# Batch 0's keys without turning: maxima turned on TensorE, a diagonal product beside identity times keys, and a new order

## The chip, the cores and the metric

One core of one Trainium2 chip runs the whole kernel. The metric is the device time of an execution in microseconds (us); less is better. The core has TensorE (PE, matrix products; PEld loads its weights), VectorE (DVE), ScalarE (ACT), GpSimd (POOL) and SyncE (SP), whose queue issues nearly all DMAs here. Each engine works through its own queue in order and waits for others by semaphores.

## What is computed

The reference is a linear attention followed by a feed-forward layer with a maximum of three products. Cut to what matters:

```
q_s = softmax(q, over the 64 columns of a head)        # 8 batches, 8 heads, 576 rows, 64 columns
k_s = softmax(k, over the 576 rows)                    # a maximum and a sum per column
kv  = einsum('bhsd,bhse->bhde', k_s, v)
x   = einsum('bhsd,bhde->bhse', q_s, kv)               # 4608 x 512 when heads stand side by side
h   = max(x @ w1, x @ w2, x @ w3)                      # 512 -> 768
out = h @ w_out                                        # 768 -> 512
```

Everything is float32. The softmax of the keys runs along the rows, which lie on the partitions of the chip's memory, so its maximum and sum go across partitions.

## The kernel before, in words

**The work and its tiles.** The 576 rows of a batch are split into 512 ("main") and 64 ("left"). Attention goes by pairs of heads: a `Pair(b, g)` has number n = 4 b + g, and m = n % 2. Two pairs, m = 0 and m = 1, together give two of the four 128-row blocks of x (blocks `cc` 0 to 3 of a batch). The feed-forward layer multiplies each f32 number as a high and a low part, three products (`L985` for the gates, `L1032` for the second layer); the weights are split into such parts in twelve "slices" (`Slices`, lines 463 to 492) by ACT, DVE and POOL at the start. Batches 0 to 2 run gate by gate (`Chunk`), batches 3 and later in couples by a scheme with seven products instead of eight (`Duo`, L1211), whose mixed weights are prepared meanwhile (`mix_weights`, L1100 to 1110, over the buffer `bdf`).

**Keys of batches 0 and 1** go through `k_turned`: TensorE turns the keys of a pair (L620 and 624 in batch 0, L611 and 614 in batch 1), so that the maximum runs along the free axis on DVE (L629, L630); ACT takes the exponential with the maximum as bias and gathers the sum (L636, L637); TensorE turns the result back (L642, L643); ACT or DVE copies it (L647, L648); TensorE multiplies it with v (L716, ten products per pair); DVE makes the reciprocal of the sum (L722, L725) and ACT scales the two 64x64 results into the diagonal blocks of a 128x128 matrix of `bdf` (L728). `bdf` is cleared once at the start (L386). From batch 2 on, `k_plain` finds the maximum across partitions with POOL's all-reduce (L660).

**Queries.** For the pairs in `Q_BY_ACT`, ACT does exponential and sum row block by row block (L757, eight instructions of 64 columns, each followed by a read of its accumulator); for the others DVE or POOL subtracts the maximum (L762), ACT takes one exponential (L786) and DVE the sums (L788). From batch 2 on, `ROWS_FROM` to `ROWS_TO` says the same for later pairs (L775 against L781, L786, L788). Normalised queries (L802) of batches 0 and 1 are turned on TensorE (L839) and copied (L843).

**x.** L858 multiplies the queries with the matrices of `bdf`; ACT copies the high part (L865); the low part is made by TensorE and ACT for the blocks in `X_BY_PE` (L868: minus identity times the high part into the same bank, L870: copy), else by DVE (L873).

**The order.** Nothing is reordered on the chip: a planner in the kernel (`Streams`) writes out the order of every engine's queue before the run. Each stream of steps has a rank; a step whose inputs are ready by the planner's own costs is issued in order of time, and among those ready at about the same time the lowest rank goes first. Steps that name two engines go to the one that ends first. The constants `AT`, `STEP` (ranks of batches 0 and 1), `FIRST`, `CHUNK`, `PAIR_STEP` (later batches), `SLICE...` (weight slices), `LEFT_AT`, `KEEP_AT`, `MIX_AT` set these ranks. `FIRST_LOADS` is the written-out order of the first loads on SP's queue: `w` a weight slice (1 MB), `k`, `q`, `v` 512 rows of a pair (256 KB), `K`, `V` the left rows of two pairs (64 KB). While TensorE has nothing ready early on, the planner fills in products of the identity by itself (L415). Rooms such as four PSUM banks `pf` (gates and, in batch 0, the small results `sm`), three banks `pa` and one `sm` bound what can be under way; `in_pf` fixes the order in which `pf` is handed out.

Of the kernel before, what the change touches and what calls it, by code (L numbers as in the profile page):

```python
# [45 lines left out]

BANKS = 3, 1

Q_BY_ACT = (0, 2, 3, 4, 5, 7)

KEEP_AFTER = 'wo'

WO_AT = 185.58

BEFORE_Y0 = 6

X_BY_PE = (1, 2, 3)
# [45 lines left out]
class Streams:  # L103
# [3 lines left out]
    def __init__(self, rooms, queued):  # L107
        self.all, self.when, self.blocked, self.left = [], {}, {}, 0
        self.queued = queued
        self.rooms = rooms  # L110
        self.taken = {}
        self.freed = {}
        self.clock = {"S": 0.72, "A": 2.2, "V": 4.0, "G": 9.0, "T": 0.0, "-": 0.0}
# [129 lines left out]
def linear_attention_then_maxout_ffn(  # L243
# [121 lines left out]
    keT = start.tile([P, S], F32, name="keT", bufs=1)  # L365
    qf = [place(f"qf{i}", [P, CH], F32, E_AT + 28672 + 2048 * i) for i in range(2)]

    minus = place("minus", [P, P], F32R, H_AT + 10240)
    nc.gpsimd.memset(adder, 0)
    nc.gpsimd.tensor_add(out=adder[:, 0:1], in0=adder[:, 0:1], in1=adder[:, 1:2])  # L370
# [23 lines left out]
    def left_rows(src, b, hs):  # L394
        return src[b, hs, CH:S].rearrange("h p d -> p h d")

    in_pf = [("sm", n) for n in range(NP)]
# [12 lines left out]
    st = Streams({"pf": 4, "pa": BANKS[0], "sm": BANKS[1], "keT": 1, "hp": NJ, "tmp": 3, "ke": 2, "kep": 1, "qe": 2, "qf": 2, "qt": 1, "tb": 1, "qT": 1, "ws": len(ws), "hs": 3}, {"pf": in_pf, "hs": in_hs, "ws": in_ws, "tb": list(range(TURNED * NP, B * NP, 2))})  # L410
    spare = sm.tile([P, CH], F32, name="sm")

    def products_for_nothing(n):
# [98 lines left out]
    class Pair:  # L512
# [89 lines left out]
        def k_turned(self):  # L602
# [44 lines left out]
            copy(out=ke[:, 0:4].rearrange("p s h d -> p (s h d)"), in_=kep)  # L647
            copy(out=ke[:LEFT, 4].rearrange("p h d -> p (h d)"), in_=kel)  # L648

        def k_plain(self):  # L650
# [24 lines left out]
            if n % 2:  # L675
                yield from self.two_products()
# [27 lines left out]
        def k_steps(self):  # L704
            n = self.n
            if not self.turned:
                yield from self.k_plain()
                return
            yield from self.k_turned()
            ke = self.ke  # L710
            yield Step("T", 0.9, [("v", n)], free=[("ke", n)], gives=("kv", n))
            kv = self.sm[:, 2 * P : 3 * P]
            for s in range(5):
                rows = slice(0, LEFT if s == 4 else P)
                for hh, r in enumerate(heads):
                    nc.tensor.matmul(  # L716
                        out=kv[r, :D], lhsT=ke[rows, s, hh, :], rhs=self.v_rest[rows, hh] if s == 4 else self.vt[rows, hh, s],
                        start=(s == 0), stop=(s == 4),
                    )
# [6 lines left out]
            yield Step("A", 0.65, free=[self.small_room()], gives=("bd", n))  # L726
            for r in heads:
                nc.scalar.activation(out=bdf[r, n, r], in_=kv[r, 0:D], func=AF.Copy, scale=rk[r])  # L728


        def q_steps(self):
# [113 lines left out]
        def x_steps(self):  # L845
# [10 lines left out]
            for m in range(2):  # L856
                for hh, r in enumerate(heads):
                    nc.tensor.matmul(  # L858
                        out=banks[hh][heads[m], :], lhsT=bdf[r, n - 1 + m, r], rhs=qf[m][r, :], start=True, stop=True
                    )  # L860
            for hh in range(2):
                cc = 2 * (self.g // 2) + hh
# [47 lines left out]
    def left_queries():  # L910
# [39 lines left out]
        for n in range(0, TURNED * NP, 2):  # L950
            b, g = divmod(n, NP)
            for m in range(2):
                for hh, r in enumerate(heads):
                    at, to = (g + m) * P + b * LEFT, g // 2 * P + b * LEFT
                    nc.tensor.matmul(
                        out=banks[hh][heads[m], to : to + LEFT], lhsT=bdf[r, n + m, r], rhs=qT[r, at : at + LEFT],
                        start=True, stop=True,
                    )
        for hh in range(2):
# [378 lines left out]
                yield Step("S", 0.68, gives=(ch, g), kb=(256, 256))  # L1338
                nc.sync.dma_start(out=to[low][0:LEFT, hs, 4, :], in_=left_rows(of[low], 0, hs))

    def landed(g):
        for ch in "kqv":
            yield Step("-", 0.0, [("%smain" % ch, g), (ch.upper(), g // 2) if ch != "q" else None], gives=(ch, g))

    st.add(first_loads(), -1000.0)
    for g in range(NP):
        st.add(landed(g), 0.0)

    def open_late():
        yield Step("-", 0.0, [("x", 0, g) for g in range(NP)], gives="late")  # L1350
# [58 lines left out]
    for (b, g), p in pairs.items():  # L1409
# [10 lines left out]
        st.add(p.k_steps(), at, step)  # L1420
# [66 lines left out]
```

## Time and profile before

| what | value |
|---|---|
| runs of the kernel before | 653.18 us median of 3 (653.03 to 654.44) |
| the profiled execution, its own time | 654.29 us |
| its span in the trace | 652.5 us |
| PE busy | 636.5 us, 98% |
| DVE, ACT, POOL busy | 431.4, 291.3, 58.0 us |
| DMA | 135.96 MB, mean 208 GB/s |

A profile describes one execution. "Busy" is the time in which an engine had an instruction under way; a busy PE is not PE at its peak. A line such as L620 is a line of the kernel before. In a timeline the columns are start, duration, engine, line, operation and shapes; in the chain of waits they are start, length, and what the end of the program was waiting for at that time. Windows list, for each stretch of the span, the busy time of each engine with the number of its instructions. All times in the text are microseconds from the start of the span unless said otherwise.

### The profile page before, as it was taken

The numbers are of one execution on the slowest core, as the hardware profiler recorded it, in microseconds if no ns is written. First come the engines' busy times: TensorE is split into PE (matmuls) and PEld (weight loads), VectorE is DVE, ScalarE is ACT, GpSimd is POOL, SyncE is SP. The second block draws the span as 40 slices with busy tenths as digits, with TensorE's granted clock in tenths as the row PEclk, the third lists the DMA queues.
The fourth block names the chain that finished last, engine by engine and source line by source line (L and its number), as shares of the span: only waits on it lengthen the run. The fifth ranks groups of instructions, "written<-read, shape, count | busy, mean of one in ns | idle before, by whom it ended". The sixth has DMA issues, their size and how long they took to land.

```text
span 652.5 us, 10284 instructions
## 1 busy us (share of the span) xinstructions
PE 636.5 (98%) x3599; PEld 509.6 (78%) x3599; DVE 431.4 (66%) x768; ACT 291.3 (45%) x713; POOL 58.0 (9%) x67
## 2 busy tenths in 40 slices
PE   6999999999999998999999999999999999999997
PEld 5768787887877777778787778778888888888885
DVE  7999987567777888988488999742436702343420
ACT  5999644266545534643244464422224522213131
POOL 1134342210010001010000011000000000000000
PEclk9999999999999999999999999999999999999999
DMA  9986477497887788899999971866663236666121
GB/s 287 365 237 224 160 252 277 128 293 216 260 266 226 203 229 222 247 297 319 315 236 265 259 208 60 245 199 193 192 193 117 78 127 190 193 193 196 39 65 64
DMA packets 137411, 135.96 MB, mean 208 GB/s; under 512 B 46608, under 2 KB 105488, under 8 KB 136208
## 3 DMA queue, kind: packets, MB, share of 16 engines
q1 hardware_dynamic: 137280, 135.17, 69.0%
q8 instruction: 29, 0.48, 0.3%
q14 instruction: 22, 0.18, 0.1%
q10 hardware_dynamic: 80, 0.13, 0.1%
HBM read 95.16 MB, written 33.03 MB: 196 GB/s over the span
## 4 chain that ended last, share of the span: by engine, by line
PE 83%; DVE 9%; DMA 5%; ACT 2%; issue 1%; POOL 0%; SPq 0%; DVEq 0%; ACTq 0%
PE pf L1211 38%; PE pf L1032 20%; PE pf L985 18%; DMA bdf<-keep_w 2%; PE pa L690 2%; DMA qt<-in_q_dram 2%; PE pa L890 2%; DVE tb L810 1%; DMA wst<-in_moe_w_dram 1%; DVE xb L1144 1%; DVE m L997 1%; PE sm L716 1%; DVE wx L472 1%; DVE xf L1148 1%; PE pa L839 0%
## 5 line engine op out<-in xcount | busy, mean ns | idle before, releaser
L1211 PE MATMUL pf<-xb,ws 128*128 128x512 f32 x1134 | 260.8, 390 | 0.2 <-DVE mm L1244 0.2
L1211 PEld LDWEIGHTS pf<-xb,ws 128*128 128x128 f32 x1134 | 212.2, 188 | 45.0 <-DVE mm L1244 0.6
L985 PE MATMUL pf<-x,wa 128*128 128x512 f32 x648 | 155.1, 394 | 0.0
L985 PEld LDWEIGHTS pf<-x,wa 128*128 128x128 f32 x648 | 119.6, 188 | 27.7 <-issue 2.4
L1240 DVE TENSOR_TENSOR mm<-pf,mm 128x512 f32<-128x512 f32 x36 | 24.9, 692 | 86.4 <-PE pf L1211 86.1
L1032 PE MATMUL pf<-oh,hs 128*128 128x512 f32 x192 | 59.3, 390 | 0.0
L1259 ACT COPY pf<-pf 128x512 f32<-128x512 f32 x27 | 15.4, 571 | 85.6 <-PE pf L1211 85.4
L1053 ACT COPY m<-pf 128x512 f32<-128x512 f32 x31 | 18.2, 586 | 59.6 <-PE pf L1032 50.9
L660 POOL PARTITION_ALL_REDUCE kma<-km x24 | 20.6, 859 | 263.9 <-DVE km L657 226.4
L1032 PEld LDWEIGHTS pf<-oh,hs 128*128 128x128 f32 x192 | 36.1, 188 | 7.6
L478 POOL TENSOR_TENSOR wx<-wx,wst 128x512 int32<-128x512 int32 x24 | 33.0, 1397 | 67.4 <-DMA vt<-in_v_dram 16.7
L1032 PE MATMUL pf<-ol,hs 128*128 128x512 f32 x96 | 37.7, 393 | 0.0
L775 ACT ACTIVATE qt<-qt,qm 128x64 f32<-128x64 f32 x81 | 27.1, 337 | 11.6 <-DVE qm L771 11.6
L1252 ACT COPY u<-pf 128x512 f32<-128x512 f32 x27 | 15.9, 587 | 34.3 <-PE pf L1211 34.1
L810 DVE STREAM_TRANSPOSE tb<-qt 128x576 f32<-128x576 f32 x24 | 30.3, 1261 | 0.2
L997 DVE TENSOR_TENSOR m<-pf,m 128x512 f32<-128x512 f32 x36 | 24.8, 688 | 8.4 <-PE pf L985 8.1
L1032 PE MATMUL pf<-oh,mix 128*128 128x512 f32 x96 | 30.2, 395 | 0.0
L1032 PE MATMUL pf<-oh,h_l 128*128 128x512 f32 x72 | 28.3, 393 | 1.3 <-DVE h_l L1004 1.3
L1032 PE MATMUL pf<-ol,h_h 128*128 128x512 f32 x72 | 28.9, 401 | 0.4 <-ACT h_h L1000 0.4
L1032 PE MATMUL pf<-oh,h_h 128*128 128x512 f32 x72 | 28.1, 390 | 0.0
L771 DVE TENSOR_REDUCE qm<-qt 128x9 f32<-128x576 f32 x24 | 17.4, 745 | 14.2 <-DMA qt<-in_q_dram 14.0
L1299 DVE TENSOR_TENSOR hs<-mm,hs 128x512 fp32r<-128x512 f32 (+1 forms) x32 | 17.1, 551 | 13.1 <-ACT hs L1297 13.0
(169 smaller groups left out, 872.1 us busy)
## 6 DMA issues: line engine op xcount, KB each, us to landing
ws<-keep_s SPq DMA_DIRECT2D x108, 256.0 KB, 3.3
ws<-keep_a SPq DMA_DIRECT2D x81, 256.0 KB, 3.2
wst<-in_moe_w_dram SPq DMA_DIRECT2D x9, 1024.0 KB, 7.4
keep_a<-wa SPq DMA_DIRECT2D x12, 768.0 KB, 6.0
keep_s<-mix SPq DMA_DIRECT2D x9, 1024.0 KB, 5.3
vt<-in_v_dram SPq DMA_DIRECT2D x56, 128.0 KB, 3.8
qt<-in_q_dram SPq DMA_DIRECT2D x24, 288.0 KB, 4.5
qT<-tb SPq DMA_DIRECT2D x96, 72.0 KB, 3.9
```

The source lines that it names most:

```text
L478: nc.gpsimd.tensor_add(out=x.bitcast(I32)[:, at], in0=x.bitcast(I32)[:, at], in1=low.bitcast(I32)[:, at])
L660: nc.gpsimd.partition_all_reduce(kma, km, P, bass_isa.ReduceOp.max)
L771: nc.vector.tensor_reduce(out=qm, in_=rows3, op=ALU.max, axis=AX.X, negate=by_act)
L775: nc.scalar.activation(out=rows3[:, s, :], in_=rows3[:, s, :], func=AF.Exp, bias=qm[:, s : s + 1], accum_out=qs[:, s : s + 1],)
L810: nc.vector.transpose(out=tb[:, self.m].rearrange("p e (c s) -> p s e c", s=QS), in_=self.qt.rearrange("p s (e c) -> p s e c", e=2),)
L985: nc.tensor.matmul(out=ps, lhsT=l[:, cc, js], rhs=r, start=(cc == 0 and t == 0), stop=(cc == NC - 1 and t == 2))
L997: nc.vector.tensor_max(out=m, in0=self.m.pop((j, i)), in1=m)
L1032: nc.tensor.matmul(out=po, lhsT=l, rhs=r[:, j, :], start=(j == 0 and i == 0), stop=(j == NJ - 1 and i == 2))
L1053: nc.scalar.copy(out=o, in_=po)
L1211: nc.tensor.matmul(out=bank[on], lhsT=w[:, k, a], rhs=x[:, b, k], start=(i == 0 and p in ("P1", "P5")), stop=(i == 5), skip_group_check=True,)
L1240: nc.vector.tensor_max(out=m, in0=bank[on], in1=m)
L1299: nc.vector.tensor_tensor(out=o[:, 1, jj], in0=mm[:, h, jj, ts], in1=o[:, 0, jj].bitcast(F32), op=ALU.subtract)
```

## The change

For batch 0, two pairs at a time: DVE or POOL takes the maximum over the row blocks within a partition (`k_most`: 512, 256 and 256 elements), TensorE turns the two 128x128 results, DVE takes the (negated) maximum along the free axis and multiplies the identity with it into `diag`. In `k_exp`, per pair, TensorE puts identity times keys into a bank and adds `same` (a matrix of ones) times `diag`, which subtracts each column's maximum on every partition; ACT takes one exponential from the bank. In `k_sums` TensorE multiplies with v, and with a column of ones for the sums; DVE makes the reciprocals and scales. No keys of batch 0 are turned, nothing is turned back and no sum is gathered on ACT. Keys of batch 1 go as before, but all 64x64 matrices now lie in columns 0 to 63 of their place in `bdf` ("matrices in one place"), so that one ACT instruction scales both, and `bdf` is no longer cleared. The small results of batch 0 take two `pf` turns instead of four. The order of the first loads, the ranks, `Q_BY_ACT`, `X_BY_PE` and `ROWS_TO` are new.

```
-FIRST, CHUNK, SLICE = 156.28, 58.31, 0.38
-PAIR_STEP, LATE_STEP = 10.68, 2.24
-AT = (91.2, -134.6, -41.9, 150.9, 228.6, 248.4, 271.1, -101.1)
-STEP = (13.73, 6.2)
-SLICES_AT, SLICE_STEP, SLICE_HI, SLICE_LO = -70.75, -0.79, 10.62, -16.13
+FIRST, CHUNK, SLICE = -26.06, 64.81, 1.49
+PAIR_STEP, LATE_STEP = 10.7, 2.75
+AT = (133.8, -45.7, -88.8, 94.7, 169.3, 289.5, 356.3, -82.3)
+STEP = (13.86, 1.0)
+SLICES_AT, SLICE_STEP, SLICE_HI, SLICE_LO = -3.29, -1.07, 14.53, -11.66
-FIRST_LOADS = 'wkqvKkkwvKVqwqkqvVv'
+FIRST_LOADS = 'wkqKkqvkvwwVqqkvVKv'
-Q_BY_ACT = (0, 2, 3, 4, 5, 7)
+Q_BY_ACT = (0, 2, 4, 5, 7)
-WO_AT = 185.58
+WO_AT = 145.21
-X_BY_PE = (1, 2, 3)
+X_BY_PE = (0, 1, 2, 4)
-ROWS_FROM, ROWS_TO = 8, 17
+ROWS_FROM, ROWS_TO = 8, 15
-LEFT_AT, KEEP_AT, PLAIN_AT, MIX_AT, MIX_STEP = 27.6, 1671.48, 53.02, 356.43, -81.06
+LEFT_AT, KEEP_AT, PLAIN_AT, MIX_AT, MIX_STEP = -26.51, 1749.35, 18.42, 378.43, -149.99
-    nc.vector.memset(bdf, 0.0)
+    nc.vector.memset(same, 1.0)
+        def k_most(self):
...
+            e = yield Step(
+                "VG", (dve(512) + 2 * dve(256), pool(512) + 2 * pool(256)), [("k", n - 1), ("k", n)], take=[("km4", n)],
+                port="VG",
+            )
...
+            unit[e].tensor_tensor(out=half4, in0=k4[:, :, 0:2], in1=k4[:, :, 2:4], op=ALU.max)
+            unit[e].tensor_tensor(out=most, in0=h4[:, :, :, 0], in1=h4[:, :, :, 1], op=ALU.max)
...
+            for i in range(2):
+                at = slice(i * P, (i + 1) * P)
+                nc.tensor.transpose(out=kmT[:, at], in_=km4[:, at], identity=ident)
...
+            nc.vector.tensor_reduce(out=km, in_=kmT.rearrange("p (m c) -> p m c", m=2), op=ALU.max, axis=AX.X, negate=True)
...
+            nc.vector.tensor_tensor(
+                out=diag, in0=ident.unsqueeze(1).broadcast_to([P, 2, P]), in1=km.unsqueeze(2).broadcast_to([P, 2, P]),
+                op=ALU.mult,
+            )
+        def k_exp(self, i):
...
+            nc.tensor.matmul(
+                out=kp, lhsT=ident, rhs=k4[:, i::2, 0:4].rearrange("p h s d -> p h (s d)"), start=True, stop=False,
...
+            nc.tensor.matmul(
+                out=kp, lhsT=same, rhs=diag[:, i].rearrange("p (h d) -> p h d", h=2).unsqueeze(2).broadcast_to([P, 2, 4, D]),
...
+            nc.scalar.activation(
+                out=ke[:, 0:4].rearrange("p s h d -> p h s d"), in_=kp.rearrange("p (h s d) -> p h s d", h=2, s=4), func=AF.Exp
+            )
+        def k_sums(self):
...
+                for s in range(5):
+                    rows = slice(0, LEFT if s == 4 else P)
+                    nc.tensor.matmul(
+                        out=kv[:, i, D : D + 1], lhsT=p.ke[rows, s].rearrange("p h d -> p (h d)"), rhs=ones[rows],
+                        start=(s == 0), stop=(s == 4),
+                    )
...
+                out=bdf[:, n - 1 : n + 1, :D], in0=kv[:, :, :D], in1=rk.unsqueeze(2).broadcast_to([P, 2, D]), op=ALU.mult
...
-            for r in heads:
-                nc.scalar.activation(out=bdf[r, n, r], in_=kv[r, 0:D], func=AF.Copy, scale=rk[r])
+            nc.scalar.activation(out=bdf[:, n, :D], in_=kv[:, :D], func=AF.Copy, scale=rk)
...
+        if b == 0 and p.m:
+            st.add(p.k_most(), at, step)
+            for i in range(2):
+                st.add(p.k_exp(i), at + (2 + i) * step, step)
+        st.add(p.k_steps(), at + (5 * step if b == 0 else 0.0), step)
```

More of the change, by code (lines that the diff above doesn't have):

```diff
@@ L366, in linear_attention_then_maxout_ffn @@
     qf = [place(f"qf{i}", [P, CH], F32, E_AT + 28672 + 2048 * i) for i in range(2)]
+    half4 = place("half4", [P, 4, 2, D], F32, H_AT)
+    km4 = place("km4", [P, 2 * P], F32, H_AT + 2048)
+    diag = place("diag", [P, 2, P], F32, H_AT + 3072)
+    same = place("same", [P, P], F32, H_AT + 4096)
     minus = place("minus", [P, P], F32R, H_AT + 10240)
@@ L395, in left_rows @@
         return src[b, hs, CH:S].rearrange("h p d -> p h d")
-    in_pf = [("sm", n) for n in range(NP)]
+    in_pf = [("sm", n) for n in range(1, NP, 2)]
     for c in range(PAIRED):
@@ L409, in linear_attention_then_maxout_ffn @@
         in_pf += [("S", c, i) for i in range(4)] + [(c, "y", t) for t in range(8)]
-    st = Streams({"pf": 4, "pa": BANKS[0], "sm": BANKS[1], "keT": 1, "hp": NJ, "tmp": 3, "ke": 2, "kep": 1, "qe": 2, "qf": 2, "qt": 1, "tb": 1, "qT": 1, "ws": len(ws), "hs": 3}, {"pf": in_pf, "hs": in_hs, "ws": in_ws, "tb": list(range(TURNED * NP, B * NP, 2))})
+    st = Streams({"pf": 4, "pa": BANKS[0], "sm": BANKS[1], "keT": 1, "km4": 1, "diag": 1, "hp": NJ, "tmp": 3, "ke": 2, "kep": 1, "qe": 2, "qf": 2, "qt": 1, "tb": 1, "qT": 1, "ws": len(ws), "hs": 3}, {"pf": in_pf, "hs": in_hs, "ws": in_ws, "tb": list(range(TURNED * NP, B * NP, 2))})
     spare = sm.tile([P, CH], F32, name="sm")
@@ new lines, in k_exp @@
+        def k_exp(self, i):
+            n, k4 = self.n, k0[:, self.four : self.four + 4]
+            p = pairs[divmod(n - 1 + i, NP)]
+            room = [("pa", ("ke", p.n))]
+            yield Step("T", f32(CH) + f32(P), [("kmT", n)], take=room)
+            kp, kl = pa.tile([P, CH], F32, name="pa"), self.sm[:LEFT, (2 + i) * P : (3 + i) * P]
+            nc.tensor.matmul(
+                out=kp, lhsT=ident, rhs=k4[:, i::2, 0:4].rearrange("p h s d -> p h (s d)"), start=True, stop=False,
+                skip_group_check=True,
+            )
+            nc.tensor.matmul(
+                out=kl, lhsT=ident[:LEFT, :LEFT], rhs=k4[:LEFT, i::2, 4], start=True, stop=False, skip_group_check=True
+            )
+            yield Step("T", f32(CH) + f32(P), [("diag", n)], free=[("diag", n)] if i else ())
+            nc.tensor.matmul(
+                out=kp, lhsT=same, rhs=diag[:, i].rearrange("p (h d) -> p h d", h=2).unsqueeze(2).broadcast_to([P, 2, 4, D]),
+                start=False, stop=True, skip_group_check=True,
+            )
+            nc.tensor.matmul(out=kl, lhsT=same[:, :LEFT], rhs=diag[:, i], start=False, stop=True, skip_group_check=True)
+            yield Step("A", act(CH) + act(P), take=[("ke", p.n)], free=room, gives=("kexp", p.n))
+            ke = p.ke = att.tile([P, 5, 2, D], F32, name="ke")
+            nc.scalar.activation(
+                out=ke[:, 0:4].rearrange("p s h d -> p h s d"), in_=kp.rearrange("p (h s d) -> p h s d", h=2, s=4), func=AF.Exp
+            )
+            nc.scalar.activation(out=ke[:LEFT, 4].rearrange("p h d -> p (h d)"), in_=kl, func=AF.Exp)
@@ new lines, in k_sums @@
+        def k_sums(self):
+            n, both = self.n, (pairs[divmod(self.n - 1, NP)], self)
+            yield Step(
+                "T", 2.5, [("kexp", n - 1), ("kexp", n), ("v", n - 1), ("v", n), ("diag", n)], free=[("ke", n - 1), ("ke", n)],
+                gives=("kv", n),
+            )
+            kv = self.sm.rearrange("p (i c) -> p i c", c=P)[:, 0:2]
+            for i, p in enumerate(both):
+                for s in range(5):
+                    rows = slice(0, LEFT if s == 4 else P)
+                    for hh, r in enumerate(heads):
+                        nc.tensor.matmul(
+                            out=kv[r, i, :D], lhsT=p.ke[rows, s, hh, :], rhs=p.v_rest[rows, hh] if s == 4 else p.vt[rows, hh, s],
+                            start=(s == 0), stop=(s == 4),
+                        )
+                for s in range(5):
+                    rows = slice(0, LEFT if s == 4 else P)
+                    nc.tensor.matmul(
+                        out=kv[:, i, D : D + 1], lhsT=p.ke[rows, s].rearrange("p h d -> p (h d)"), rhs=ones[rows],
+                        start=(s == 0), stop=(s == 4),
+                    )
+            yield Step("V", 0.35)
+            rk = att.tile([P, 2], F32, name="rk2", bufs=2)
+            nc.vector.tensor_scalar_add(out=rk, in0=kv[:, :, D], scalar1=1e-9)
+            nc.vector.reciprocal(out=rk, in_=rk)
+            yield Step("V", dve(2 * D) + 0.05, gives=("bd", n), free=[self.small_room()])
+            nc.vector.tensor_tensor(
+                out=bdf[:, n - 1 : n + 1, :D], in0=kv[:, :, :D], in1=rk.unsqueeze(2).broadcast_to([P, 2, D]), op=ALU.mult
+            )
+            yield Step("-", 0.0, gives=("bd", n - 1))
@@ L708, in k_steps @@
                 return
+            if self.b == 0:
+                if self.m:
+                    yield from self.k_sums()
+                return
             yield from self.k_turned()
@@ L725, in k_steps @@
             nc.vector.reciprocal(out=rk, in_=rk)
[L726 to L728 removed]
+            yield Step("A", 0.35, free=[self.small_room()], gives=("bd", n))
+            nc.scalar.activation(out=bdf[:, n, :D], in_=kv[:, :D], func=AF.Copy, scale=rk)
         def q_steps(self):
@@ L858, in x_steps @@
                     nc.tensor.matmul(
-                        out=banks[hh][heads[m], :], lhsT=bdf[r, n - 1 + m, r], rhs=qf[m][r, :], start=True, stop=True
+                        out=banks[hh][heads[m], :], lhsT=bdf[r, n - 1 + m, :D], rhs=qf[m][r, :], start=True, stop=True
                     )
@@ L955, in left_queries @@
                     nc.tensor.matmul(
-                        out=banks[hh][heads[m], to : to + LEFT], lhsT=bdf[r, n + m, r], rhs=qT[r, at : at + LEFT],
+                        out=banks[hh][heads[m], to : to + LEFT], lhsT=bdf[r, n + m, :D], rhs=qT[r, at : at + LEFT],
                         start=True, stop=True,
@@ L1339, in first_loads, with landed @@
                 nc.sync.dma_start(out=to[low][0:LEFT, hs, 4, :], in_=left_rows(of[low], 0, hs))
-    def landed(g):
-        for ch in "kqv":
-            yield Step("-", 0.0, [("%smain" % ch, g), (ch.upper(), g // 2) if ch != "q" else None], gives=(ch, g))
+    def landed(g, ch):
+        yield Step("-", 0.0, [("%smain" % ch, g), (ch.upper(), g // 2) if ch != "q" else None], gives=(ch, g))
     st.add(first_loads(), -1000.0)
     for g in range(NP):
-        st.add(landed(g), 0.0)
+        for ch in "kqv":
+            st.add(landed(g, ch), 0.0)
     def open_late():
```

14 lines of the change are left out of this document (12 added, 2 removed).

## The prediction

> **What bounds the kernel now.** I read the page's span first, then the busy times by stretches, then the busy time of line 415 alone, and last the chain of waits.
>
> ```profile
> span 652.5 us, 10284 instructions
> ```
>
> ```profile
> 10.00:35.00 25.00, 21.90 (x240) 17.31 (x240) 22.02 (x49) 22.78 (x83) 6.51 (x7) 1.00 1.08 349
> 35.00:61.00 26.00, 25.56 (x180) 19.47 (x178) 24.64 (x45) 25.26 (x83) 8.05 (x8) 1.00 0.79 244
> 61.00:220.00 159.00, 158.81 (x976) 125.95 (x973) 121.19 (x220) 85.36 (x265) 30.73 (x36) 1.00 0.71 225
> 220.00:290.00 70.00, 66.76 (x385) 51.12 (x384) 63.18 (x117) 32.66 (x61) 5.42 (x6) 1.00 0.86 247
> 290.00:648.40 358.40, 358.33 (x1802) 290.70 (x1800) 193.01 (x320) 122.03 (x223) 7.04 (x8) 1.00 0.62 182
> ```
>
> The columns are the stretch, its length, and the busy time of PE, PEld, DVE, ACT and POOL. From 61 us on, PE is a queue that is always full: it idles 0.19 us up to 220, 3.24 us from 220 to 290 and 0.07 us up to 648.4. What happens early is therefore passed on to the end as long as the stretch at 220 to 290 lets it through. Before 61 us, PE's busy time is partly filler: products of the identity by itself (line 415) that are issued while nothing else is ready.
>
> ```profile
> 10.00:35.00 25.00, 8.83 (x61) 7.30 (x60) 1.00 1.08 349
> ```
>
> So of the 25 us from 10 to 35, PE works 21.90 - 8.83 = 13.07 us and has 11.9 us free; the 26 us from 35 to 61 hold eight records of filler, 0.89 us (the row at 38.68 further down), so 24.7 of work and 1.3 free. What sets the moment of the first gate product is DVE and ACT: 22.02 + 22.78 of 2 x 25 us busy, and 24.64 + 25.26 of 2 x 26 in the stretch behind it. The chain that ended last, in order of time, shows them one after the other up to the first x:
>
> ```profile
> 22.43 0.60 DVE ke L647
> ...
> 23.97 0.75 DVE keT L630
> ...
> 30.66 0.31 ACT bdf L728
> 30.99 0.78 ACT keT L636 x2
> ...
> 33.88 0.70 DVE x L873
> ```
>
> The first four rows are work on batch 0's keys that lies on this chain (line 647 copies the turned-back keys, 630 finds a maximum, 728 scales, 636 is the exponential): 0.60 + 0.75 + 0.31 + 0.78 = 2.44 us, and not all of it is shown. The last row is the low part of the first x, 0.70 us on DVE; the first gate product comes when it is written, at 34.6 to 35.
>
> **The change, part by part.** Prices are the step from one start to the next, where the engine ran on without a gap.
>
> *TensorE.*
>
> ```profile
> 38.68 0.89 PE sm L415 x8
> ...
> 42.96 1.02 PE pa L858 x8
> ...
> 47.45 0.88 PE sm L716 x20
> ```
>
> ```profile
> 15.23 0.66 PE L642 MATMUL pa<-ident,keT 128*128 128x128 f32 x4
> ...
> 15.93 1.09 PE L620 MATMUL pa<-ident,k 128*64 128x128 f32 x16
> ...
> 17.21 0.71 PE L415 MATMUL sm<-ident 128*128 128x128 f32 x4
> ```
>
> The old way costs per pair 17.21 - 15.93 = 1.28 us (turning the keys), 15.93 - 15.23 = 0.70 (turning back) and 0.88 (line 716): 2.86, and 11.4 for four pairs. The new products are in f32 with a moving side of 512 and 128 columns, which the trace doesn't have in this form. Ten products of line 716 show as 20 records, so one f32 product of 128 columns by 128 is two records of line 415, 2 x 0.89 / 8 = 0.22 us, and by columns one of 512 is 0.89. The other bound is line 858, four products of 512 columns in quarters of the array in 1.02 us, 0.26 each (it is also the x of pairs 2 and 3). The full array is line 415's form, so I take 0.89 + 0.22. For two pairs: identity by keys and `same` by `diag`, 2 x 2 x 1.11 = 4.44; two transposes 0.22; the sums over v 2 x 0.88 = 1.76; ten products with `ones` of one column, 20 records between nothing and 0.11 each, nearest to line 716's 0.88 / 20 = 0.044, so 0.9. That is 7.3, and 14.6 for the batch: 3.2 us more than before (with the ends, from 4.9 less to 5.8 more). One more low part of x goes over PE (X_BY_PE has four instead of three), at most 0.89. All of this is hidden by the 11.9 + 1.3 us that PE has free before 61 us, as long as it is issued there; if that cover is gone, it is 3.2 to 4 us on the end.
>
> *VectorE.*
>
> ```profile
> 21.75 0.68 DVE L788 TENSOR_REDUCE qs<-qe 128x8 f32<-128x512 f32 x1
> 22.34 0.69 DVE L647 COPY ke<-pa 128x512 f32<-128x512 f32 x1
> ...
> 28.20 0.69 DVE L647 COPY ke<-pa 128x512 f32<-128x512 f32 x1
> ...
> 28.99 0.20 DVE L629 TENSOR_REDUCE km<-pf 128x1 f32<-128x64 f32 x1
> ...
> 29.91 0.08 DVE L630 DVE_READ_ACCUMULATOR2_ANT km<- 128x1 f32 x1
> ```
>
> Old: maximum 29.91 - 28.99 = 0.92 per pair, copy 28.99 - 28.20 = 0.79 for two of the four pairs: 5.3 us. New, per two pairs: one maximum over 512 elements, 22.34 - 21.75 = 0.59 by the nearest row; two over 256 and the diagonal product, also 256.
>
> ```profile
> 216.27 0.42 DVE L1100 TENSOR_TENSOR bdf<-bdf 128x256 f32<-128x256 f32 x1
> 216.61 0.69 DVE L997 TENSOR_TENSOR m<-pf,m 128x512 f32<-128x512 f32 x1
> ...
> 217.99 0.76 DVE L781 TENSOR_TENSOR qt<-qt,qm 128x576 f32<-128x576 f32 x1
> 218.66 0.15 DVE L697 TENSOR_SCALAR rk<-pa 128x2 f32<-128x2 f32 x1
> ```
>
> The first two rows give 0.34 for 256 elements; the reduction of 256 lies between line 629's 0.20 (64 elements) and 0.59 (512), I take 0.40; the scaling of 128 is below 0.34, I take 0.25. Sum 0.59 + 3 x 0.34 + 0.40 + 0.25 = 2.26, twice 4.5: 0.8 us saved. The small reciprocals become two sets instead of four; I leave them at nothing. Pair 3's queries leave ACT's row-by-row form (Q_BY_ACT loses 3), which adds a subtraction and a sum on DVE, 2 x 0.59 = 1.2. X_BY_PE gains 0, and 4 for 3: one low part less, -0.70. Net: -0.3 us. The clearing of `bdf` at the start is dropped for a smaller memset; it lies in the time in which the weights are awaited, so nothing.
>
> GpSimd may take the three maxima instead, at the planner's choice. A row says that it isn't free of charge: line 802's product, which elsewhere has about line 788's length, took twice that when GpSimd was in its integer additions (first fence DVE, second POOL).
>
> ```profile
> 43.82 1.46 DVE L802 TENSOR_TENSOR qe<-qe,qs 128x512 f32<-128x512 f32 x1
> ```
>
> ```profile
> 42.17 2.55 POOL L478 TENSOR_TENSOR wx<-wx,wst 128x512 int32<-128x512 int32 x2 [5.88 <-DVE km L629]
> ```
>
> [...]
>
> *ScalarE.*
>
> ```profile
> 14.41 0.68 ACT L636 ACTIVATE keT<-pa,km 128x512 f32<-128x512 f32 x1
> ...
> 15.37 1.15 ACT L463 ACTIVATE wx<-wst 128x1024 f32<-128x1024 f32 x1
> ...
> 20.56 0.63 ACT L786 ACTIVATE qe<-qe 128x512 f32<-128x512 f32 x1
> 21.08 1.18 ACT L482 ACTIVATE wst<-wst 128x1024 int32<-128x1024 uint32 x1
> 22.15 0.34 ACT L757 ACTIVATE qe<-q,qm 128x64 f32<-128x64 f32 x1
> ...
> 24.81 1.03 ACT L486 CAST wa<-wx 128x1024 fp32r<-128x1024 f32 x1
> ```
>
> Old: exponential and its sums 15.37 - 14.41 = 0.96, scaling two times 0.31 per pair (line 728 in the chain), and two copies at 0.79 (DVE's row, the nearest shown): 4 x 1.58 + 1.58 = 7.9 us. New: one exponential of 512 without a sum, 21.08 - 20.56 = 0.52, and one of 128 below the 0.31 of line 728's scaling, I take 0.27: 3.2. Saved 4.7. Pair 3's queries: 24.81 - 22.15 = 2.66 becomes 0.52, 2.1 saved. Batch 1 scales with one instruction for two: 4 x 0.31 = 1.2. The additional low part over PE costs a copy, 0.52. Net: -7.5 us.
>
> *Sum for the start.* If nothing is rebalanced, the head shrinks by DVE's 0.3 us. If the planner's choices (which of ACT and DVE takes the sign bits, the copies) even both engines out, it is (7.5 + 0.3) / 2 = 3.9. The chain's rows alone say: 2.44 of keys and 0.70 of x leave it, and 2.26 of new DVE work, that of two pairs, comes in their place: 0.9, a floor, since not all that leaves is shown. I take 2.2, between the bounds.
>
> *The order of loads.* The sequence is written out anew. The last rows of keys 2 and 3 (`K`, second) were tenth and are now 18th of 19, where the second `V` stood, whose row this is:
>
> ```profile
> L1339 SPq DMA_DIRECT2D v<-in_v_dram x2: 596/602/607, 7.8 to 15.1; - x2
> ...
> DMA to landing us min/median/max: 6.4/7.8/8.1
> ```
>
> Issued at about 15.1 and landed 6.4 to 8.1 us later, they are there at 21.5 to 23.2. Keys 2 and 3 can't begin earlier. The x of pairs 2 and 3 was multiplied at 42.96; from 23 it has 20 us left, and its DVE, PE and ACT work is 2.26 + 7.3 + 1.6 + 1.0 = 12.2. Nothing, then, unless other work goes first (below).
>
> *The later order.* Ranks of all batches, mixes and slices change, and two pairs of queries (15 and 16) leave ACT's form: on DVE 2 x (0.67 + 0.67) = 2.7 us more, by line 781's row (218.66 - 217.99). Their place was just ahead of 220; DVE is busy 121.19 of the 159 us before that, which covers it. If they fall behind 220, up to 2.7 us is lost; if the new order removes the waits there, 3.24 is won. I take nothing.
>
> Sum: 652.5 - 2.2 = 650.3 us of span. The profiled execution took 654.29 us, 1.79 more than its span, and is 1.1 above the median of the runs shown, 653.18. From the median I forecast 651.0.
>
> **Rivals.**
> *Both engines even out and the waits go.* 3.9 at the start and half of the 3.24: 653.18 - 5.5 = 647.7. For it: ACT loses most, and ACT and DVE have several pieces that either can take. Against it: it asks PE to do 3.2 us more in a head that is shorter by 3.9, from 13.2 free to 6.1, with every piece ready in time.
> *The gain is eaten at 220 to 290.* DVE is busy 63.18 of 70 us there. If its work ends when it did, PE only comes earlier and waits longer: 653.2. Against it: keys and values of those batches are loaded into buffers that PE's own products free, so this work moves up with PE.
> *Slower: x of pairs 2 and 3 comes late.* The weight slices have lower ranks than these keys (the first -3.3 and 1.5 more for each next, the keys 94.7), so DVE may take slices first. PE's gates go through x 0 to 3 in order over four banks, 24 products, and then everything behind them waits. A slice costs DVE at least these three rows:
>
> ```profile
> 7.00 0.70 DVE wx L467
> 7.72 0.70 DVE wx L468
> 8.45 1.23 DVE wx L472
> ```
>
> That is 2.63 us. The 20 us of time less 12.2 of work leave 7.8, so three slices ahead of the keys (7.9) are the point from which it decides; a fourth costs 4 x 2.63 - 7.8 = 2.7, less the 0.70 of x: 655.2. For it: the load in 18th place, and the 7.3 us of PE for these two pairs then fall behind the first gate. Against it: ACT, which loses most, can take the sign bits, and the planner puts a step where its engine is free first.
> *The keys go the new way, but f32 products at 0.89 are wrong* (0.26): no different end, since they are covered.
>
> **Numbers.** Forecast 0.48 (its own range 649.2 to 652.9), even-out 0.16, eaten 0.13, slower 0.23. A measurement here tells about 0.2% (1.3 us) from nothing. Faster: the forecast less 0.03, and 0.16, with a little from the eaten case: 0.63. Same 0.13; slower 0.24. The range 647.0 to 655.5 takes in the centres of all four.
>
> **What would show it.** Right: the first gate product at 32 to 33.5 us, fewer filler records before 61 us, ACT's busy time up to 61 us some 7 us lower, new f32 products with 0.22 us between starts per record pair of 128 columns, and PE again without a gap from 61 to 220. Wrong: a PE wait for x of pairs 2 and 3 after 35 us, PE idle clearly over 3.2 us between 200 and 300, or a first gate no earlier than 35.

## The result, and the profile after

The changed kernel takes 662.1 us (median; 660.49 to 664.08) against 653.81 us before: 1.0122 times as long, with a 95% interval of 1.0077 to 1.0166. It is slower, where a gain of 2.2 us was forecast. The page of the changed kernel (the second row is the TensorE clock that was granted, in tenths of full speed, for 40 equal slices):

```profile
span 662.2 us, 10107 instructions
...
PEclk9798999999999999999999999999999999999999
```

The second and the fourth slice are not at full clock; before, all 40 showed a 9. The stretches of the prediction, for the changed kernel (the columns as there; the third number from the end is the granted clock):

```profile
10.00:35.00 25.00, 22.29 (x125) 13.99 (x125) 17.40 (x33) 13.17 (x40) 5.58 (x5) 0.73 1.04 332
35.00:61.00 26.00, 24.18 (x162) 15.74 (x161) 19.51 (x39) 20.01 (x56) 5.07 (x4) 0.95 0.61 192
61.00:220.00 159.00, 159.00 (x993) 125.94 (x993) 125.04 (x228) 86.79 (x256) 36.99 (x39) 1.00 0.73 226
220.00:290.00 70.00, 70.00 (x431) 54.43 (x430) 64.57 (x119) 31.56 (x56) 3.41 (x4) 1.00 0.83 235
290.00:658.10 368.10, 366.83 (x1804) 297.54 (x1803) 198.73 (x328) 125.62 (x229) 6.10 (x8) 1.00 0.62 183
```

DVE went from 22.02 to 17.40 us of the 25 from 10 to 35, and ACT from 22.78 to 13.17. That is more than was forecast, since part of the work only came later: up to 61 us the changed kernel has taken five weight slices through their last step on DVE before GpSimd's additions (line 476), the kernel before six (line 472), and over the whole span DVE is busy 432.0 us against 431.4. PE is busy 22.29 of the 25 us, but at a clock of 0.73. From 61 to 290 it never idles (before, 3.43 us), and behind that it idles 1.27 us (before, 0.07). So the waits behind 61 us became fewer, and the loss comes from what lies ahead of that or from work that PE now has to do. The chain of waits gives its size, first before, then after; each time the row at which the second layer of batch 0 begins, and the last long piece of the second layer:

```profile
120.40 8.84 PE pf L1032 x39
...
617.29 31.05 PE pf L1032 x135
```

```profile
131.40 7.48 PE pf L1128 x33
...
627.00 31.05 PE pf L1128 x135
```

The second layer begins 11.0 us later; the end comes 9.7 later. The whole loss is thus there when the second layer begins, and up to it both kernels have done the same 288 records of gate products. What TensorE did until its first gate product (line 1081), in the timeline of the changed kernel:

```profile
3.96 6.08 PE L419 MATMUL sm<-ident 128*128 128x128 f32 x38 [3.96 <-DVE ident L385]
12.74 0.44 PE L674 MATMUL pf<-ident,km 128*128 128x128 f32 x2 [2.71 <-DVE km L666]
...
15.29 2.08 PE L692 MATMUL pa<-k,ident 128*128 128x512 f32 x2
...
18.50 1.91 PE L700 MATMUL pa<-diag,same 128*128 128x512 f32 x2
...
24.77 1.36 PE L729 MATMUL pf<-ones,ke 128*128 128x1 f32 x10
...
26.94 1.67 PE L729 MATMUL pf<-ones,ke 128*128 128x1 f32 x10
```

```profile
36.63 2.30 PE L1081 MATMUL pf<-x,wa 128*128 128x512 f32 x9
...
38.99 1.02 PE L700 MATMUL pa<-diag,same 128*128 128x512 f32 x2
...
43.14 0.66 PE L935 MATMUL pa<-ident,qe 128*128 128x128 f32 x4
...
45.96 0.95 PE L723 MATMUL pf<-v,ke 128*64 128x64 f32 x20
...
50.29 0.96 PE L1081 MATMUL pf<-x,wa 128*128 128x512 f32 x3
...
57.10 0.63 PE L935 MATMUL pa<-ident,qe 128*128 128x128 f32 x4 [1.38 <-DVE qs L886]
```

Three things are to be seen. TensorE sat idle for 2.71 us, waiting for the first maxima; the last step of these on DVE (line 666) took 1.53 us at 11.15, while GpSimd was in its integer additions, and 0.42 at 30.50. An f32 product of 512 columns (a pair of records of line 692 or 700) took 2.08 and 1.91 us early on and 1.02 at 38.99. And the products with the column of ones (line 729) took 1.36 and 1.67 us per pair. The granted clock in three stretches:

```profile
14.00:21.00 7.00, 7.00 (x15) 2.33 (x13) 5.85 (x13) 4.18 (x5) 0.00 (x0) 0.51 1.11 336
28.00:35.00 7.00, 7.00 (x31) 5.10 (x32) 4.64 (x11) 2.60 (x7) 0.00 (x0) 0.53 0.92 286
58.00:62.00 4.00, 3.83 (x12) 2.84 (x13) 3.93 (x7) 2.18 (x4) 0.27 (x1) 0.57 0.72 209
```

It is at half for some 6.8 us twice (the second time from just before 28) and for 3.4 us once. In the kernel before, the first gate product (line 985) and the one piece of batch 0's keys behind it (line 716) are these:

```profile
35.04 0.94 PE L985 MATMUL pf<-x,wa 128*128 128x512 f32 x3
35.91 0.95 PE L716 MATMUL pf<-v,ke 128*64 128x64 f32 x20
36.79 0.50 PE L868 MATMUL pa<-x,minus 128*128 128x512 f32 x1
```

The arithmetic up to the second layer is then: first gate product 36.63 - 35.04 = 1.6 us later; keys of pairs 2 and 3 behind it, from 38.99 to 43.14 and from 45.96 to 50.29, 8.5 us where there was one piece of 0.88: 7.6 more; and 1.8 left over, in which the third stretch at half clock lies. Why those keys come so late is shown by DVE's queue:

```profile
28.71 0.16 DVE L735 TENSOR_SCALAR rk<-pf 128x2 f32<-128x2 f32 x1 [2.36 <-PE pf L729]
...
29.32 0.68 DVE L664 TENSOR_TENSOR half<-k 128x512 f32<-128x512 f32 x1
```

The maximum of pairs 2 and 3 (line 664) stands behind the reciprocal of pairs 0 and 1 (735), which waits 2.36 us for the products with ones. DVE takes them in the order that the planner wrote. The x of pairs 2 and 3 came at 52.43 instead of 42.96:

```profile
52.43 1.09 PE L954 MATMUL pa<-qf,bdf 64*64 64x512 f32 x8
```

### The profile page after: what moved, and what is told of

Read it like the earlier page. It is cut to its first block, busy times and chain, and to the rows that moved or that the text cites. A ratio compares the mean times of both kernels' runs of the same rounds, so it can differ in the third digit from the quotient of the medians.

```text
span 662.2 us, 10107 instructions
## 1 busy us (share of the span) xinstructions
PE 648.3 (98%) x3546; PEld 513.5 (78%) x3546; DVE 432.0 (65%) x764; ACT 281.4 (42%) x644; POOL 57.4 (9%) x65
## 4 chain that ended last, share of the span: by engine, by line
PE 95%; DMA 2%; DVE 1%; ACT 1%; issue 0%; ACTq 0%
PE pf L1307 38%; PE pf L1081 23%; PE pf L1128 23%; PE pa L783 2%; PE pa L986 2%; DMA ws<-keep_s 1%; PE sm L419 1%; PE pf L729 1%; DMA wst<-in_moe_w_dram 1%; PE pa L954 1%; PE pa L692 1%; PE pa L700 1%; PE pa L935 1%; PE pf L723 1%; PE sm L813 0%
## 5 line engine op out<-in xcount | busy, mean ns | idle before, releaser
L482 POOL TENSOR_TENSOR wx<-wx,wst 128x512 int32<-128x512 int32 x24 | 35.2, 1488 | 78.4 <-DVE wx L476 20.6
L1348 ACT COPY u<-pf 128x512 f32<-128x512 f32 x27 | 15.9, 587 | 33.5 <-PE pf L1307 33.4
L871 ACT ACTIVATE qt<-qt,qm 128x64 f32<-128x64 f32 x63 | 21.1, 337 | 13.2 <-DVE qm L867 13.2
```

The costliest lines, as they stand in the source:

```text
L482: nc.gpsimd.tensor_add(out=x.bitcast(I32)[:, at], in0=x.bitcast(I32)[:, at], in1=low.bitcast(I32)[:, at])
L871: nc.scalar.activation(out=rows3[:, s, :], in_=rows3[:, s, :], func=AF.Exp, bias=qm[:, s : s + 1], accum_out=qs[:, s : s + 1],)
```

## The experiments

Three theories: "clock" (idle time and thin work let the granted clock fall), "work" (the new f32 products lie among the gates, where PE has no free time), "order" (the new ranks and loads are worse). Each run is compared with runs of the kernel before on the same chip, whose medians were 653.42 to 654.22 us; the ratio to them is given behind each time. "Order held" means that every engine's queue keeps its order, so that the planner can't change anything else.

**More fillers ahead of the first maxima.** The rest of the order is held.

```
-        n = int((min(b, SPARE[1]) - a) / (0.225 * COLD[1])) if a < SPARE[1] else 0
+        n = int((min(b, SPARE[1]) - a) / (0.225 * 1.1)) if a < SPARE[1] else 0
```

> The changed kernel with more filler products (identity by itself) ahead of the first turned maxima, 28 instead of 17 by the planner's count, so that TensorE has no idle time from 10.0 to 12.7 us; the rest of the order is the same. Theory 'clock' (the 2.7 us of idle time let the granted clock fall to 0.5 from 14 to 20.5 us, which delays all that follows): granted clock 1.0 up to 27 us, first x about 3 us earlier, time 2 to 4 us below the changed kernel's 662. Theory 'work' (the new f32 products of pairs 2 and 3 simply lie among the gates): within 1 us of 662. Theory 'order' (ranks and loads are worse): within 1 us of 662.

Measured: 663.93 us, 1.0149 times before (1.0121 to 1.0178). The windows:

```profile
14.00:21.00 7.00, 7.00 (x39) 3.60 (x40) 6.40 (x15) 5.87 (x9) 0.00 (x0) 1.00 1.12 323
24.00:31.00 7.00, 7.00 (x32) 5.13 (x33) 4.64 (x11) 3.54 (x13) 0.76 (x1) 0.52 1.08 384
```

The first stretch is at full clock now, and the first gate product came 3.2 us earlier (33.41, below). The half clock after the products with ones stayed. The time did not improve, against the 2 to 4 us that "clock" expected: no gain from the first gap alone can be told. In the profiled execution the second layer did begin 3.2 us earlier (128.19 against 131.40), but the span was only 0.3 us shorter (661.9 against 662.2). From 140 to 350 us PE idled 2.56 us, in the changed kernel 1.20; what took the rest is not shown. So a gain in the head need not reach the end. The timeline at full clock also gives the prices:

```profile
31.69 1.02 PE L692 MATMUL pa<-k,ident 128*128 128x512 f32 x2
32.64 0.43 PE L696 MATMUL pf<-k,ident 64*64 64x128 f32 x2
33.00 0.66 PE L935 MATMUL pa<-ident,qe 128*128 128x128 f32 x4
33.41 2.30 PE L1081 MATMUL pf<-x,wa 128*128 128x512 f32 x9
...
43.62 1.36 PE L729 MATMUL pf<-ones,ke 128*128 128x1 f32 x10
44.91 0.95 PE L723 MATMUL pf<-v,ke 128*64 128x64 f32 x20
```

A product of 512 columns costs 32.64 - 31.69 = 0.95 us, the small one beside it 33.00 - 32.64 = 0.36, and the five products with ones of a pair 44.91 - 43.62 = 1.29. In the timeline of the changed kernel, where the same step is 1.29 (46.83 to 48.12), the weight loads of the five (PEld, ten records) are busy for 1.28 us of it.

**Without the products with ones** (the sums of batch 0's keys are left out, a column of the product stands in for them); order held.

```
-                    nc.tensor.matmul(
-                        out=kv[:, i, D : D + 1], lhsT=p.ke[rows, s].rearrange("p h d -> p (h d)"), rhs=ones[rows],
-                        start=(s == 0), stop=(s == 4),
-                    )
-            nc.vector.tensor_scalar_add(out=rk, in0=kv[:, :, D], scalar1=1e-9)
+            nc.vector.tensor_scalar_add(out=rk, in0=kv[:, :, 0], scalar1=1e-9)
```

> The changed kernel without the 20 products with the column of ones (the sums of batch 0's keys are left out, a column of the product takes their place). Theory 'clock' (their one-column stream counts as little activity and brings the second stretch at half clock, 28 to 34.5 us): no such stretch, 3 us for the clock and 2.7 to 5.4 us for the products themselves, time 655 to 657. Theory 'work': the products alone, 2.7 us of pairs 2 and 3 and perhaps 2.7 of pairs 0 and 1, time 657 to 660, with the half clock after 28 us still there. Theory 'order': 661 to 662.

Measured: 656.41 us, 1.0036 (1.0011 to 1.0061). In the trace the clock is not at half where the products with ones had stood, but it is from 47 to 54 us (0.50 to 0.55 in windows of 1 us), behind a wait of 1.63.

> Both: more fillers ahead of the first maxima and no products with the column of ones (sums left out). Theory 'clock': granted clock 1.0 up to 55 us and 650 to 654. Theory 'work': 657 to 660. Theory 'order': 660 to 662.

Measured, with the fillers as well: 655.56 us, 1.0029 (1.0008 to 1.0050). Most of the loss is gone. In the profiled execution the view's granted clock is 1.00 throughout, and:

```profile
29.66 2.30 PE L1075 MATMUL pf<-x,wa 128*128 128x512 f32 x9
...
47.78 0.63 PE L929 MATMUL pa<-ident,qe 128*128 128x128 f32 x4 [1.61 <-DVE qs L880]
48.86 0.66 PE L615 MATMUL pa<-ident,kt 128*128 128x128 f32 x4 [0.45 <-ACT x L960]
```

```profile
121.73 7.48 PE pf L1122 x33
```

The first gate product comes 5.4 us earlier than in the kernel before, at 29.66, and yet the second layer begins 1.3 us later (121.73 against 120.40). The windows show DVE and ACT:

```profile
10.00:35.00 25.00, 24.26 (x162) 15.56 (x161) 22.45 (x43) 17.57 (x46) 5.83 (x6) 1.00 1.09 346
35.00:61.00 26.00, 23.94 (x180) 17.07 (x180) 23.81 (x42) 23.01 (x72) 9.91 (x8) 1.00 0.78 247
```

DVE is busy 46.26 us in the two stretches, 0.4 less than before, and ACT 40.58, 7.5 less, while as many weight slices as before (six) have passed their last step on DVE ahead of GpSimd's. That is close to the forecast's 0.3 and 7.5. So ACT was relieved and the first gate product came early (how much of that is the new order is not separated), and the f32 products that are left behind the first gate product (32.03 to 36.17 and 38.99 to 40.74, 5.9 us where there was 0.88), together with the two waits in the rows above, used it up.

The profiled execution was the fastest of eight (654.10 us) and the only one with a mean clock of 0.999; the others had 0.993 to 0.997 and took 654.21 to 657.70. So the clock can still be a part of the 0.29% that is left.

**One filler behind each product with ones** (pairs 0 and 1), on top of the first experiment.

```
                         start=(s == 0), stop=(s == 4),
                     )
+                    if n == 1:
+                        products_for_nothing(1)
```

> As e1_fill (more fillers ahead of the first maxima), and behind each of the ten products with the column of ones for pairs 0 and 1 one more filler (identity by itself, 0.22 us, 2.2 us in all); the sums are all there. Theory 'ones stream too little' (the one-column products let the clock fall to 0.5 from 24 to 31 us in e1_fill): the granted clock stays 1.0 up to 50 us and the first gate product comes 0 to 2 us earlier than e1_fill's 33.4 us in spite of 2.2 us more products. Theory 'any dense f32 work' (the half clock there has another cause, such as the place in time): the stretch at 0.5 is still there and the first gate is 2 us later, at 35.5. Time in both cases 660 to 665, as what is won up to 130 us was given back in e1_fill.

Measured: 662.51 us, 1.0138 (1.0123 to 1.0153).

```profile
24.00:31.00 7.00, 7.00 (x67) 5.54 (x67) 2.54 (x8) 3.54 (x17) 1.88 (x2) 1.00 1.06 358
```

The clock stays at 1.00 where it was 0.52, with more products in the same place: here it was the thin stream of the one-column products that brought it down, and not the place in time. But the first gate product came at 34.06, no earlier than the 33.41 of the first experiment, since the fillers take what the clock gives, and the time stayed. The clock at this place alone doesn't explain the loss.

**Ones added to the kernel before**, its order held exactly; the result is not used.

```
+            for s in range(5 if self.b == 0 else 0):
+                rows = slice(0, LEFT if s == 4 else P)
+                nc.tensor.matmul(
+                    out=self.sm[:, 3 * P : 3 * P + 1], lhsT=ke[rows, s].rearrange("p h d -> p (h d)"), rhs=ones[rows],
+                    start=(s == 0), stop=(s == 4),
+                )
```

> The kernel before, its order held exactly, with five products with the column of ones added behind the products with v of each of batch 0's pairs (their result is not used). They take 1.3 us a pair, 5.2 in all. Theory 'ones cost time and clock': three of the four lie before the first gate product, where TensorE has idle time and fillers, so 1.3 us on the path for the last and some more if the granted clock falls; 654.5 to 658. Theory 'the order alone': no more than the 1.3 us, clock 1.0 throughout, 653.5 to 655.

Measured: 656.67 us, 1.0044 (1.0024 to 1.0064), 2.9 us more, with a stretch at half clock that the kernel before didn't have:

```profile
26.00:30.00 4.00, 4.00 (x21) 3.67 (x20) 1.94 (x7) 1.87 (x8) 0.00 (x0) 0.57 1.12 363
```

**GpSimd adds the row blocks first**, so that one product with ones per pair is left; order held, fillers as in the first experiment.

```
+                nc.gpsimd.tensor_add(out=khalf[:, i], in0=flat[:, : 2 * P], in1=flat[:, 2 * P : 4 * P])
+                nc.gpsimd.tensor_add(out=ksum[:, i], in0=khalf[:, i, :P], in1=khalf[:, i, P:])
+                nc.gpsimd.tensor_add(out=ksum[:LEFT, i], in0=ksum[:LEFT, i], in1=flat[:LEFT, 4 * P :])
...
+                nc.tensor.matmul(out=kv[:, i, D : D + 1], lhsT=ksum[:, i], rhs=ones, start=True, stop=True)
```

> As e1_fill, order held, but GpSimd adds the five row blocks of the exponentials first (three additions per pair, some 1.3 us on an engine that idles there), so that one product with the column of ones per pair is left instead of five. Theory 'ones cost time and clock': no half clock from 24 to 31 us, first gate near 30 us instead of 33.4, time 656 to 659 against e1_fill's 664 (e7_fill_no_ones, without any: 655.6). If GpSimd's additions come late or hold up DVE: 660 to 664.

Measured: 659.31 us, 1.0081 (1.0056 to 1.0106): about half of what leaving them out gives.

```profile
22.20 1.32 POOL L724 TENSOR_TENSOR ksum<-khalf 128x128 f32<-128x128 f32 x1
```

```profile
24.09 0.51 PE L735 MATMUL pf<-ones,ksum 128*128 128x1 f32 x2 [1.19 <-POOL ksum L725]
24.47 2.05 PE L421 MATMUL sm<-ident 128*128 128x128 f32 x8
```

An addition of 128 columns took up to 1.32 us on GpSimd, TensorE waited 1.19 for it, and the fillers behind it ran at half clock (granted 0.50 from 25 to 27; 2.05 us for eight, against 0.89 for eight in the kernel before): the expected full clock was a miss. The first gate product came at 31.19.

**Fewer f32 products.** On top of "fillers and no ones", pairs 2 and 3 leave out identity times keys (their exponential is that of the maximum alone).

```
+            if n == 1:
                 nc.tensor.matmul(
                     out=kp, lhsT=ident, rhs=k4[:, i::2, 0:4].rearrange("p h s d -> p h (s d)"), start=True, stop=False,
...
```

> As e7_fill_no_ones (more fillers ahead, no products with the column of ones), and for pairs 2 and 3 also without the products of the identity with the keys (the exponential there is that of the maximum alone; the order is held): two f32 products of 512 columns and two small ones, 2.8 us that lie among the gates. Theory 'work' (with the ones and the clock gone, what is left of the loss is f32 products of pairs 2 and 3 behind the first gate): e7_fill_no_ones less 2 to 3 us, 652 to 654, not slower than before. Theory 'order' (what is left comes from later waits): 655 to 656, no change from e7_fill_no_ones.

Measured: 654.57 us, 1.0009 (0.9992 to 1.0026). The loss is no longer told from nothing, but neither is the difference from 1.0029, since the intervals overlap, and 654.57 lies between the ranges of the two theories. It agrees with "work" and doesn't prove it. The clock may play into this run too: its three executions with a mean clock of 0.999 or more took 651.61 to 653.99 us, the nine others (0.993 to 0.997) 654.00 to 656.60.

**The kernel before without fillers.**

```
-        if n > 0 and not self.taken.get("sm"):
+        if False:
```

> The kernel before without any filler products. Theory 'clock': TensorE idles often before 35 us, the granted clock is 0.5 for most of 10 to 35 us, and since the path there is set by DVE and ACT with TensorE's short products between them, 2 to 5 us are lost (655 to 659). Without a part of the clock: 653 to 654.

Measured: 657.37 us, 1.0063 (1.0045 to 1.0081). The granted clock shows two stretches at half, the windows of 4 us around them:

```profile
27.00:31.00 4.00, 4.00 (x39) 3.09 (x38) 2.85 (x9) 3.94 (x16) 0.00 (x0) 0.57 1.08 393
37.00:41.00 4.00, 4.00 (x28) 3.05 (x27) 3.90 (x8) 3.98 (x12) 1.13 (x1) 0.57 0.28 61
```

Ahead of 27 us this view shows 1.00, but the products don't bear that out: the 16 records of line 620, which turn the keys of one pair, took 1.91 us in the chain of waits at 16.77, as long as at 28.57 in the first of the two stretches; in the kernel before they took 1.02 (from their start at 15.93 to the next product at 16.95). So TensorE was slow at 16.77 as well.

**The order.** The old keys with all constants of the new order, and the new keys with all constants of the old one (both edits are the block of constants in the diff of the change, and with it the time at which the planner lets GpSimd start, 9 or 10 us):

> The kernel before with all the new order's constants (ranks, order of the first loads, who takes which queries and low parts), but batch 0's keys turned as before. Theory 'order': the loss stays, 658 to 663. Theories 'clock' and 'work' (the loss is in the new products and in what they leave idle): 650 to 656, and no stretch at half clock.

Measured: 672.5 us, 1.0286 (1.0249 to 1.0323).

> The changed kernel (new keys of batch 0, matrices in one place) with all constants of the order before: ranks, first loads, who takes which queries and low parts. Theory 'products' (the ones, 2.6 us per two pairs, and the f32 products cost the path what they take, wherever they stand): 657 to 664, first y product at 127 to 132 us. Theory 'order' (the new ranks, not the products, are what is worse): 650 to 655.

Measured: 671.37 us, 1.0279 (1.0260 to 1.0298). Both mixtures are worse than either kernel and than every range expected: with the old keys and the new order, PE idles 9.75 us from 220 to 350. The constants belong to their keys, and the two effects don't add up. The next two runs show how touchy the order is. Both are the kernel before with the matrices in one place; they differ in the cost that the planner is told.

```
-            yield Step("A", 0.65, free=[self.small_room()], gives=("bd", n))
-            for r in heads:
-                nc.scalar.activation(out=bdf[r, n, r], in_=kv[r, 0:D], func=AF.Copy, scale=rk[r])
+            yield Step("A", 0.35, free=[self.small_room()], gives=("bd", n))
+            nc.scalar.activation(out=bdf[:, n, :D], in_=kv[:, :D], func=AF.Copy, scale=rk)
```

> The kernel before with only the matrices in one place: one scaling on ACT for two (8 times 0.3 us less on ACT), no clearing of bdf; keys, ranks and loads as before, but the planner may order differently since the step is shorter. Theory 'products': the loss is in the new keys, so 651 to 654. Theory 'order is touchy' (any shift in the planner's times gives another order, and what is won in the head is given back at 220 to 350 us): 654 to 658.

Measured: 664.84 us, 1.0180 (1.0163 to 1.0197), above both ranges expected.

> As e6_before_one_place, but the planner is told the old cost of the scaling step (0.65 us), so that the order of every engine is that of the kernel before to the instruction; only the eight scalings are one instruction instead of two, and bdf is not cleared. Theory 'the order is touchy' (e6_before_one_place lost 11 us by its new order alone): 652 to 654, at most 1.5 us better than before. Theory 'the matrices in one place cost something on the chip': 660 to 666 as in e6_before_one_place.

Measured, with `Step("A", 0.65, ...)` kept: 653.2 us, 0.9992 (0.9975 to 1.0009). The windows, first with 0.35 and then with 0.65:

```profile
61.00:140.00 79.00, 76.70 (x460) 59.03 (x458) 57.70 (x87) 33.07 (x63) 23.81 (x28) 1.00 0.59 197
220.00:290.00 70.00, 63.21 (x393) 48.13 (x392) 61.78 (x110) 32.90 (x70) 3.20 (x4) 0.98 0.85 242
```

```profile
61.00:140.00 79.00, 78.91 (x459) 62.48 (x459) 58.79 (x96) 37.30 (x80) 24.92 (x29) 1.00 0.65 218
220.00:290.00 70.00, 68.19 (x395) 53.17 (x394) 63.71 (x116) 32.25 (x56) 4.44 (x5) 1.00 0.89 248
```

With 0.35 PE idles 2.3 us from 61 to 140 and 6.8 from 220 to 290, half of the latter in one wait:

```profile
286.65 8.68 PE L1209 MATMUL pf<-xb,ws 128*128 128x512 f32 x30 [3.36 <-DVE xb L1142]
```

Here it is the low part of a converted x (line 1142 on DVE) that came 3.36 us late. The matrices in one place cost and bring nothing that can be told; a 0.3 us difference in the planner's belief moved the time by 11.6 us (664.84 against 653.2).

## Why the prediction was wrong, step by step

- *"All of this is hidden by the 11.9 + 1.3 us that PE has free before 61 us, as long as it is issued there"* is the step that failed. The free time lay mostly ahead of the first gate product, and the keys of pairs 2 and 3 were issued behind it: 8.5 us among the gates, where PE has no free time. The text named the condition and its price (3.2 to 4 us) and gave it as one reason for the slower rival, but made no rival of it. That the products then came among the gates is shown by the timeline; that those with ones, with what they do to the clock and to DVE's wait, are most of the loss is shown by the runs without them (1.0149 became 1.0029).
- *7.3 us for two pairs* was mis-sized. At full clock the four large products take 0.95 to 1.06 us each in the first experiment's timeline (0.89 taken), the four small ones 0.36 (0.22 taken) and the products with ones 2.58 (0.9 taken); with 0.22 for the transposes and 1.76 with v as forecast that is 10.0. For the batch this is 20.0, 8.6 us more than the old 11.4, and above the forecast's upper end of 5.8 more. The row of line 716 was the wrong neighbour for the ones: their ten weight loads of 128 columns fill 1.28 of the 1.29 us per pair (in the changed kernel at 46.83), so a record costs 0.13 us instead of 0.044.
- *The clock* was in no term. The profile before showed 1.00 everywhere, and I didn't ask what kept it there. The kernel before without fillers answers it: 0.63% slower, with two stretches at half clock (0.57 in each window of 4 us) and slow products before them (1.91 us where 1.02 was). In the changed kernel the clock fell behind an idle time of 2.71 us (0.51 from 14 to 21 us), and with the idle time filled it stayed at 1.00 there; in the run with GpSimd's additions it fell behind a wait of 1.19 us (0.50 from 25 to 27); and a busy PE with one-column products lost it too (0.52 from 24 to 31 us in the first experiment).
- *DVE and ACT are relieved, 2.2 us at the start*: the mechanism agrees with the runs. With the ones out of the way and the clock at 1.00, ACT is busy 7.5 us less up to 61 us and DVE 0.4 less, close to the forecast, and the first gate product came at 29.66, 5.4 us earlier; the new order has a share in that which no run separates. But TensorE was then the bound, against which the forecast checked only a sum of free time. "First gate product at 32 to 33.5 us" failed in the changed kernel (36.63). Of the other signs, there were fewer fillers (27 records against 69 from 10 to 61 us), PE had no gap from 61 to 220, and ACT's busy time up to 61 us fell by 14.9 us instead of 7, partly because work was put off.
- *The slower rival* had the right place (x of pairs 2 and 3 later than 42.96: 52.43) and the wrong mechanism: not weight slices ahead of the keys on DVE, but the reciprocal, waiting for the ones. Its 655.2 was too little. The load in 18th place is not what they waited for: it was issued at 14.64, loads of its line landed at most 9.6 us behind their issue, and DVE began at 29.32.
- *The later order, taken as nothing*: 3.24 us of waits from 220 to 290 became none, and 1.2 more came behind. That is a gain of 2.0 in the profile, in the direction of its bound; the gain was not eaten there.
- *A gain eaten at 220 to 290* didn't happen in the changed kernel. In one of the planner's other orders (cost 0.35) PE idled 6.8 us there.

What stays open: whether some order of the new keys beats the kernel before. With the order held and the same fillers, the ones, their clock and DVE's wait for them cost 8 us together (663.93 against 655.56), and how the 8 us divide among the three is not shown; the rest of the loss, 0.3%, could be the f32 products, the order or the clock, and the run that takes some of the products away doesn't decide it. No version that beats both kernels was found.

## What to carry to other kernels

Free time of an engine is worth something only ahead of the point from which that engine is the bound: place every added product on the timeline before calling it hidden. Price a product with one moving column by its weight load (here 1.28 of the 1.29 us of ten records), and remember that it may cost the clock as well (here 0.52 instead of 1.00 for 7 us); the same sum by an addition elsewhere has its own wait (here 1.19 us). Where a planner writes the order, test a local change with the planner's beliefs held, and only then let it plan anew.

## What the runs showed of the hardware

In the first experiment twenty records of one-column f32 products (two groups of ten, at 21.55 and 23.72 us, with products of 64 columns around them) brought the granted clock to half for 6.8 us (0.52 from 24 to 31 us), although PE counted as busy for 7.00 of these 7.00 us; one 128-column product behind each kept it at 1.00 there. It fell behind idle times too, but not behind all: behind 2.71 us in the changed kernel (0.51 from 14 to 21) and behind 1.19 us in the run with GpSimd's additions (0.50 from 25 to 27). With nearly the same wait, the run without ones and with more fillers kept its clock (1.61 us at 47.78; 1.00), while the one without ones and with the old fillers lost it (1.63 us at 47.17; 0.50 to 0.55 from 47 to 54). So the length of a wait alone doesn't tell what it does to the clock.

Worked out from the granted clock in windows of 1 us (0.55 taken as half clock for nine tenths of the window), the changed kernel's three stretches begin at 14.1, 27.8 and 58.5 and last 6.8, 6.8 and 3.4 us; the first experiment's two begin at 24.2 and 55.0 and last 6.8 and 3.4. What sets these times and lengths is not shown by any run.

The runs of one kernel differ by up to 3 us either way of their median (the kernel before: 651.12 to 656.66 us, median 653.75).
